# Moving one early load to another DMA queue, two 1/sqrt to ScalarE, and two pauses into a matmul fill list

## The chip, the cores and the metric

The kernel runs on one core of one Trainium2 chip. The metric is the device time of one execution in microseconds (us). Executions of one kernel differ by 1 to 2 us of 550 (549.82 to 551.59 in 20 runs of the kernel before), which is more than this change is about; so a time is given as the median of several runs and, for comparisons, as a ratio. A ratio is the mean time of one kernel's fast runs over the mean time of the other's fast runs of the same rounds on the same chip, so it is not quite the ratio of the medians quoted beside it.

Engine names in the profile: PE is TensorE (matmul), PEld its weight loads, DVE is VectorE, ACT is ScalarE, POOL is GpSimd. SPq and ACTq are the sequencers that issue DMAs on the SP and the ACT queue.

## The reference, cut to what matters

```python
xn = _layernorm(x)                      # 2048 tokens x 512
s  = attention(xn @ wq, k, v) @ wo      # 32 heads, 8 kv heads, the last 512 keys of the cache
g  = _silu(_silu(xn @ w1) @ w2)         # w1 512 x 1792, w2 1792 x 512
return x + s * g
```

## The kernel before

The tokens are worked in four blocks of 512 (four tiles of 128). At the start, block 0 is normalised and goes through the first MLP layer alone. Seven pairs of 128-wide chunks of w1 are run on tiles 0, 1 (`half` 0), then the same seven pairs on tiles 2, 3 (`half` 1):

```python
nc.sync.dma_start(x_blk[0][0:HP4, 0, :], ...)      # tile 0, half of the partitions
nc.scalar.dma_start(x_blk[0][HP4:P, 0, :], ...)    # the other half, ACT queue
# ... the same for tile 1
nc.sync.dma_start(w1_sb[0][:, :, 0 : NE // 2], ...)        # first w1 piece, 256 KB
nc.sync.dma_start(w1_sb[0][:, :, NE // 2 : NE], ...)       # second w1 piece, 256 KB
nc.scalar.dma_start(x_blk[0][:, 2:4, :], ...)              # tiles 2, 3, 256 KB, ACT queue
nc.sync.dma_start(w1_sb[0][:, :, NE:], ...)                # third w1 piece, 384 KB
nc.sync.dma_start(w1_sb[1][:, :, 0:NE], ...)               # w1's second half, 512 KB
# ... further loads, all on the SP queue
# tiles 0, 1: stats, 1/sqrt on ScalarE, center, transposes on PE
nc.scalar.activation(scratch, scratch, ACT.Tanh)   # brings the Tanh table in
stats(0, 2); stats(0, 3)
rstd_of(2, 2)                                      # 1/sqrt of tiles 2, 3 on POOL
center(0, 2); center(0, 3)
for i in range(2 * FH):
    h_pair(i, i // FH)       # 8 matmuls; then Tanh on ScalarE, multiply on VectorE
    if i == 3:               # transposes of tiles 2, 3 and their copies to xnT
        t2 = turn(2); t3 = turn(3)
        nc.scalar.copy(xnT[0][:, :, 2 * P : 3 * P], t2)
        nc.vector.tensor_copy(xnT[0][:, :, 3 * P : 4 * P], t3)
# ... queries for the first two heads are made between the last pairs
```

Then comes one long loop over 4 x 32 heads (queries, scores, exp, transposes by DMA, values). Its matmuls are interleaved with "fill" units taken from a list: the rest of the MLP while block 0 runs, the output projection later.

```python
fill = []
for b in range(NBLK):
    hs, os_ = mlp_units(b, lambda i: "f")   # first layer (4 units a chunk), second layer (14 a tile)
    fill += hs * (b > 0) + os_
def pump(n):
    for _ in range(n):
        if fill:
            fill.pop(0)(); done += 1
```

The first unit of each chunk needs one of two PSUM buffers ("f"), which comes free when VectorE has evacuated what was in it: the chunk before the last or, for the first chunks of block 1, a tile of block 0's second layer (its result is `gate`).

The softmax here doesn't subtract the row's maximum and nothing guards it: scores larger than these inputs give would overflow.

## Time and profile before

| | before |
|---|---|
| median of 20 runs | 550.57 us (549.82 to 551.59) |
| the profiled run, its span | 551.54 us, 549.3 us |
| first MLP matmul starts | 7.34 us |
| first score matmul starts (the long loop begins) | 23.09 us |
| last matmul starts | 545.24 us |

From the page of the kernel before (busy time of each engine, share of the span, instructions):

```profile
span 549.3 us, 8536 instructions
...
PE 543.1 (99%) x2676; PEld 261.7 (48%) x2676; DVE 458.5 (83%) x1258; ACT 392.3 (71%) x1125; POOL 20.7 (4%) x41
...
PE 96%; DMA 1%; DVE 1%; SPq 0%; issue 0%; ACT 0%
```

PE is the bound; the last line is the chain of work that ended last. A small change can only win where PE stands still. The waits of PE in the same trace (engine, line, what it waited for: us in all, times, longest):

```profile
PE warm_ps L635 <- DVE eps L74: 1.2, 1, 1.2
PE h_ps L683 <- DMA w_0_111<-in_B_w_dram: 1.0, 1, 1.0
PE h_ps L148 <- DVE gate_414 L190: 0.2, 1, 0.2
```

"Busy" ends of matmuls are modelled, so I measure waits from start to start: a 512-column matmul starts 0.216 us after the one before (0.108 for 256 columns), and what a start is later than that is called a *gap* below. Two stretches of the timeline of the kernel before (start, duration, engine, line, what, count, and in brackets the idle time before it with what ended it):

```profile
1.97 0.61 ACTq L617 DMA_DIRECT2D x_119<-in_A_x_dram  x1
2.25 0.59 SPq L615 DMA_DIRECT2D w_0_111<-in_B_w_dram  x1
...
3.98 0.51 SPq L619 DMA_DIRECT2D w_1_112<-in_B_w_dram  x1
...
7.31 1.28 ACT L667 ACT_TABLE_LOAD   x1
7.34 0.68 DVE L109 BATCH_NORM_STATS2 st<-x_119 128x6 f32<-128x512 bf16 x1
7.34 1.91 PE L683 MATMUL h_ps<-xnT_107,w_0_111 128*128 128x256 bf16 x16
...
8.71 1.17 ACT L691 ACTIVATE th<-h_ps 128x512 bf16<-128x512 f32 x2
9.13 0.23 POOL L114 TENSOR_SCALAR rstd<-mv 128x2 f32<-128x2 f32 x1 [7.82 <-DVE mv L110]
9.44 0.72 POOL L115 TENSOR_TENSOR rstd<-rstd,neg_half 128x2 f32<-128x2 f32 x1
...
10.23 1.49 PE L683 MATMUL h_ps<-xnT_107,w_0_111 128*128 128x256 bf16 x12 [0.98 <-DMA w_0_111<-in_B_w_dram]
...
13.61 0.42 DVE L702 COPY xnT_107<-t_ps 128x512 bf16<-128x512 bf16 x1
...
15.24 3.22 PE L683 MATMUL h_ps<-xnT_107,w_0_111 128*128 128x256 bf16 x28
...
42.53 0.38 PE L148 MATMUL h_ps<-xnT_108,w_0_111 128*128 128x512 bf16 x1
43.08 0.38 PE L148 MATMUL h_ps<-xnT_108,w_0_111 128*128 128x512 bf16 x1 [0.18 <-DVE gate_414 L190]
43.30 0.38 PE L233 MATMUL sc_ps<-kT_91,qT 128*128 128x512 bf16 x1
```

At 10.23 PE has waited for the third w1 piece (gap 1.15 us); at 11.72 for w1's second half (gap 0.17). At 43.08 the second chunk of block 1 has waited for a PSUM buffer (0.55 us since the start before it, so a gap of 0.34). One more gap, 0.18 us, is at 112.98. From 11.84 us to the last matmul no other gap is longer than 0.06 us. The matmuls of the second half (15.24) need the two copies of tiles 2, 3, which are done in time.

### The profile page before, as it was taken

The page shows a single profiled execution, that of the slowest core. Times are in us where ns is not written, and L with a number is a line of the kernel's source. Part 1 is how long each engine was busy: PE and PEld are TensorE (multiplying, and loading weights), DVE is VectorE, ACT ScalarE, POOL GpSimd, SP SyncE. Part 2 cuts the span into 40 slices and gives each one's busy share as a digit, 9 for nine tenths or more (in the row PEclk, how much of TensorE's full clock was granted, in tenths as well). Part 3 has the DMA queues.
Part 4 walks back from the last instruction along what each step waited for, and adds up shares of the span by engine and source line. Part 5 has one row for each costly group of instructions (what it writes and reads, how often), then busy time and mean ns, then how long its engine had stood idle before and what let it go on. Part 6 is the DMA issues. An engine that isn't in the chain of part 4 may idle for free.

```text
span 549.3 us, 8536 instructions
## 1 busy us (share of the span) xinstructions
PE 543.1 (99%) x2676; PEld 261.7 (48%) x2676; DVE 458.5 (83%) x1258; ACT 392.3 (71%) x1125; POOL 20.7 (4%) x41
## 2 busy tenths in 40 slices
PE   8999999999999999999999999999999999999997
PEld 5644444444444444444444444444444444444586
DVE  5878878977786688898889888988889889988897
ACT  5558757866786677777777777777788888888600
POOL 1000010000000000010001000100010000100010
PEclk9999999999999999999999999999999999999999
DMA  8969669697759799979887988797878878988931
GB/s 257 257 114 201 144 133 175 147 166 141 165 97 184 172 220 218 204 152 184 165 147 157 183 161 146 155 191 156 151 158 181 153 153 157 189 153 154 173 78 39
DMA packets 298925, 89.69 MB, mean 163 GB/s; under 512 B 282368, under 2 KB 297984, under 8 KB 298880
## 3 DMA queue, kind: packets, MB, share of 16 engines
q1 hardware_dynamic: 297136, 85.09, 79.0%
q0 software_dynamic: 1312, 3.67, 2.6%
q10 hardware_dynamic: 432, 0.39, 0.3%
q8 instruction: 21, 0.34, 0.2%
q14 instruction: 24, 0.20, 0.1%
HBM read 17.30 MB, written 2.10 MB: 35 GB/s over the span
## 4 chain that ended last, share of the span: by engine, by line
PE 96%; DMA 1%; DVE 1%; SPq 0%; issue 0%; ACT 0%
PE o_ps L275 20%; PE q_ps L211 20%; PE sc_ps L233 20%; PE s_ps L332 15%; PE oB_ps L180 8%; PE h_ps L148 7%; PE m_ps L470 4%; PE h_ps L683 2%; DMA w_0_111<-in_B_w_dram 1%; DVE gate_414 L190 0%; DVE p_all L248 0%; DVE st L109 0%; SPq L612 0%; DVE qT L223 0%; SPq L615 0%
## 5 line engine op out<-in xcount | busy, mean ns | idle before, releaser
L236 ACT ACTIVATE p_all<-sc_ps 128x512 bf16<-128x512 f32 x512 | 305.3, 597 | 104.4 <-PE sc_ps L233 100.4
L248 DVE TENSOR_SCALAR p_all<-p_all,rden 128x512 bf16<-128x512 bf16 x512 | 157.9, 351 | 9.1
L281 DVE CAST oT<-o_ps 128x512 bf16<-128x512 f32 x128 | 88.2, 689 | 35.8 <-PE o_ps L275 35.2
L236 ACT ACTIVATION_READ_ACCUMULATOR p_all<-sc_ps 128x1 f32 x512 | 100.3, 196 | 0.0
L233 PEld LDWEIGHTS <-qT 128*128 128x128 bf16 x512 | 50.1, 98 | 60.8 <-issue 0.5
L223 DVE CAST qT<-q_ps 128x512 bf16<-128x512 f32 x111 | 76.3, 687 | 3.2 <-PE q_ps L211 3.2
L332 PEld LDWEIGHTS <-oT 128*128 128x128 bf16 x384 | 37.6, 98 | 45.3
L246 DVE RECIPROCAL rden<-den 128x2 f32<-128x2 f32 x256 | 40.5, 158 | 11.2 <-ACT p_all L236 11.0
L158 ACT ACTIVATE th<-h_ps 128x512 bf16<-128x512 f32 x42 | 25.0, 595 | 4.0 <-PE h_ps L148 3.9
L332 PE MATMUL s_ps<-wo_big_2085,oT 128*128 128x512 bf16 x84 | 26.0, 379 | 0.0
L332 PE MATMUL s_ps<-wo_big_2345,oT 128*128 128x512 bf16 x84 | 26.0, 379 | 0.0
L332 PE MATMUL s_ps<-wo_big_2346,oT 128*128 128x512 bf16 x84 | 26.0, 379 | 0.0
L332 PE MATMUL s_ps<-wo_big_2084,oT 128*128 128x512 bf16 x84 | 26.0, 379 | 0.0
L233 PE MATMUL sc_ps<-kT_91,qT 128*128 128x512 bf16 x64 | 24.3, 379 | 0.0
L233 PE MATMUL sc_ps<-kT_92,qT 128*128 128x512 bf16 x64 | 24.3, 379 | 0.0
L233 PE MATMUL sc_ps<-kT_93,qT 128*128 128x512 bf16 x64 | 24.3, 379 | 0.0
L233 PE MATMUL sc_ps<-kT_94,qT 128*128 128x512 bf16 x64 | 24.3, 379 | 0.0
L233 PE MATMUL sc_ps<-kT_95,qT 128*128 128x512 bf16 x64 | 24.3, 379 | 0.0
L233 PE MATMUL sc_ps<-kT_96,qT 128*128 128x512 bf16 x64 | 24.3, 379 | 0.0
L233 PE MATMUL sc_ps<-kT_97,qT 128*128 128x512 bf16 x64 | 24.3, 379 | 0.0
L233 PE MATMUL sc_ps<-kT_98,qT 128*128 128x512 bf16 x64 | 23.9, 379 | 0.0
L349 POOL DMA_DIRECT2D out_dram<-x_e x12 | 6.6, 549 | 313.9 <-DVE rden L246 257.6
(316 smaller groups left out, 872.3 us busy)
## 6 DMA issues: line engine op xcount, KB each, us to landing
pT<-p_all SPq DMA_TRANSPOSE x128, 4.4
x_e<-in_A_x_dram POOLq DMA_DIRECT2D x12, 128.0 KB, 3.3
out_dram<-x_e POOLq DMA_DIRECT2D x12, 128.0 KB, 2.2
w_0_113<-in_B_w_dram SPq DMA_DIRECT2D x1, 896.0 KB, 10.2
w_1_114<-in_B_w_dram SPq DMA_DIRECT2D x1, 896.0 KB, 9.5
w_0_111<-in_B_w_dram SPq DMA_DIRECT2D x2, 256.0 KB, 4.2
w_1_112<-in_B_w_dram SPq DMA_DIRECT2D x1, 512.0 KB, 7.7
x_131<-in_A_x_dram SPq DMA_DIRECT2D x1, 512.0 KB, 10.6
```

What stands on the lines that cost most here:

```text
L148: nc.tensor.matmul(h_ps[:, lo : lo + n], w1_sb[f // FH][:, c, (f % FH) * P : (f % FH + 1) * P], xnT[b][:, c, lo : lo + n], start=(c == 0), ...
L158: nc.scalar.activation(th, h_ps, ACT.Tanh, scale=0.5)
L180: nc.tensor.matmul(cur["ps"], hT[b][f // 2][:, f % 2, j * P : (j + 1) * P], w2_sb[f // FH][:, f % FH, :], start=(f == 0), stop=(f == NFC - 1),
L211: nc.tensor.matmul(cur["ps"], wq_sb[h // REP][:, c, (h % REP) * DH : (h % REP + 1) * DH], xnT[b][:, c, :], start=(c == 0), stop=(c == ND - 1),
L223: nc.vector.tensor_copy(qT[s], cur["ps"])
L233: nc.tensor.matmul(sc, qT[s][:, j * P : (j + 1) * P], kT[h // REP], start=True, stop=True)
L236: nc.scalar.activation(p_all[s][:, :, j, :], sc.rearrange("p (kc q) -> p kc q", q=P), ACT.Exp, scale=INV_SQRT_DH, accum_out=den[s][:, j : ...
L246: nc.vector.reciprocal(rden, den[s][:, j0 : j1 + 1])
L248: nc.vector.tensor_scalar_mul(p_all[s][:, :, j, :], p_all[s][:, :, j, :], rden[:, j - j0 : j - j0 + 1])
L275: nc.tensor.matmul(cur["ps"], v_sb[h // REP][:, kc, :], pT[s][:, kc, :], start=(kc == 0), stop=(kc == NKC - 1))
L281: nc.vector.tensor_copy(oT[s // 2][:, s % 2, :], cur["ps"])
L332: nc.tensor.matmul(acc[j], oT[(b * HQ + h) // 2][:, h % 2, j * P : (j + 1) * P], wo_of(h), start=(h == 0), stop=(h == HQ - 1),)
```

## The change

The intent, as I read it: let the first two w1 pieces arrive undisturbed by tiles 2, 3; since those then come late, take their 1/sqrt on ScalarE, for which the Tanh table has to come in behind it (a load of 1.28 us); and fill the wait at 43 us with a score matmul.

```diff
-        nc.scalar.dma_start(x_blk[0][:, 2:4, :], x0v[:, 2:4, :])
+        nc.sync.dma_start(x_blk[0][:, 2:4, :], x0v[:, 2:4, :])
 ...
-        nc.scalar.activation(scratch, scratch, ACT.Tanh)
         stats(0, 2)
         stats(0, 3)
-        rstd_of(2, 2)
-        center(0, 2)
-        center(0, 3)
+        for j in range(2, 4):
+            rstd_first(j)
+            center(0, j)
+        nc.scalar.activation(scratch, scratch, ACT.Tanh)
 ...
-            fill += hs * (b > 0) + os_
+            if b > 0:
+                fill += hs[:ND] + [None] * 2 * (b == 1) + hs[ND:]
+            fill += os_
 ...   # pump: a None takes a turn and runs nothing
```

More of the change, by code (lines that the diff above doesn't have):

```diff
@@ L721, in pump @@
                 if fill:
-                    fill.pop(0)()
+                    u = fill.pop(0)
                     done += 1
+                    if u is not None:
+                        u()
         wo_plan = {
```

## The prediction

> **What bounds the kernel.** PE: the page gives PE 543.1 of 549.3 us (99%), the chain of waits is 96% PE, and full-width matmuls follow each other every 0.215 us. In the timeline PE loses time in four places: start-up until the first MLP matmul at 7.34 us; 1.25 us between starts at 10.23, where the waits name the third w1 piece (landed 10.18); about 0.17 us extra at 11.72 (first piece of w1's second half, landed 11.68); and 0.34 us extra at 43.08, where the second h chunk of block 1 waits for a gate on DVE that ends at 43.03. The change can win under 2 us of 550.
>
> **What the change does.**
> 1. x tiles 2, 3 (256 KB) leave the ACT queue (issued 1.97, landed 5.23) and go behind the second w1 piece on the SP queue. The first two w1 pieces (landed 6.08, 7.43) come some tenths earlier, but PE did not wait for them. The third piece and the next have the same bytes ahead of them as before. The Trainium skill ("DMA: Bandwidth & Descriptors", rules for kernel authors) says that spreading DMAs over issuing engines brings no bandwidth, since they share 16 DMA engines; the trace agrees (DMA share 1.05, 341 GB/s from 7.3 to 12.6 us). I expect 10.2 and 11.7 us again, within 0.3: the 1.25 us wait stays. x tile 1 (landed 4.28) may land 0.1 to 0.25 earlier, which lengthens that wait by as much.
> 2. Tiles 2, 3 now land at about 7.5 to 8.1 us; DVE took them up at 7.34 anyway, so their statistics start 0.2 to 0.7 later.
> 3. Two POOL operations (0.23 + 0.72 us) go; two ScalarE activations of 0.29 us come. The centred tiles are ready near 10.3 us (before: 10.94); PE transposes them only at 12.17: no gain.
> 4. The Tanh table load (1.28 us) moves from 7.31 to behind the second 1/sqrt, about 9.8 to 10.1. The first MLP Tanh moves from 8.71 to about 11.4. Four Tanh/DVE pairs at 0.6 + 0.69 us then run before the copies of the transposed tiles; the DVE copy ends near 15.1 to 15.5 (before: 14.03), and PE needs it at 15.24. Loss 0 to 0.4 us, say 0.15.
> 5. The pauses put one score matmul (0.215 us) between the first and second h chunk of block 1. The 0.34 us stall shrinks to about 0.1: gain about 0.2. The order of fills against exponentials shifts by two slots; there PSUM buffers come free 0.05 to 0.4 us before use: small stalls may come or go: +-0.2.
>
> **Sum.** -0.2 (pause) + 0.15 (late table) - 0.15 (start-up, order) = -0.2: **550.5 us, 80% range 549.6 to 551.3.** Chances: faster by over 2% 0.005, within 2% 0.99, slower by over 2% 0.005.
>
> **What the profile would show.** Step 1: PE waits for the third w1 piece until 10.0 to 10.5 and starts the next piece's weights at 11.5 to 12.0. Step 2: statistics of tile 2 start at 7.5 to 8.1, behind a DMA wait. Step 4: table load near 10, first Tanh near 11.4; a PE gap of up to 0.4 us near 15.3 blamed on an xnT copy. Step 5: PE wait at the gate near 43 us at most 0.15 us.
>
> **What would make it wrong.** If the separate ACT queue slowed the weights (the slowest DMA engine finished the third w1 piece 1.2 us after the other fifteen), the piece could come earlier and win up to 1 us. If x lands after 8.5, the Tanh chain is later still and PE stalls over 0.5 us. If the shifted order stalls every turn of block 1's h chunks, 0.5 us more is lost.

## The result, and the profile after

The full change ran in 551.08 us (median of 10 runs, 550.66 to 552.33) against 550.57 us (20 runs): ratio 1.0012, 95% interval 1.0004 to 1.0021. It is within 2%, and slightly slower: about 0.66 us (0.0012 x 550.57). From the page of the changed kernel:

```profile
span 549.5 us, 8535 instructions
...
PE 542.7 (99%) x2676; PEld 261.1 (48%) x2676; DVE 458.6 (83%) x1258; ACT 392.1 (71%) x1127; POOL 19.5 (4%) x39
...
PE 97%; DVE 1%; DMA 1%; ACT 1%; SPq 0%; issue 0%; ACTq 0%
```

The waits of PE after the change:

```profile
PE warm_ps L635 <- DVE eps L74: 1.2, 1, 1.2
PE h_ps L683 <- DMA w_0_111<-in_B_w_dram: 0.9, 1, 0.9
PE h_ps L683 <- DVE xnT_107 L702: 0.6, 1, 0.6
PE h_ps L683 <- DMA w_1_112<-in_B_w_dram: 0.2, 1, 0.2
```

The wait for the gate is no longer listed; a wait for the copy of tile 3 (L702) is new. The timeline of the changed kernel, the lines that answer to those above:

```profile
2.24 0.59 SPq L615 DMA_DIRECT2D w_0_111<-in_B_w_dram  x1
...
3.44 0.51 SPq L617 DMA_DIRECT2D x_119<-in_A_x_dram  x1
...
4.50 0.51 SPq L619 DMA_DIRECT2D w_1_112<-in_B_w_dram  x1
...
6.55 1.91 PE L683 MATMUL h_ps<-xnT_107,w_0_111 128*128 128x256 bf16 x16
8.20 0.69 DVE L109 BATCH_NORM_STATS2 st<-x_119 128x6 f32<-128x512 bf16 x1 [1.67 <-DMA x_119<-in_A_x_dram]
...
9.34 1.49 PE L683 MATMUL h_ps<-xnT_107,w_0_111 128*128 128x256 bf16 x12 [0.88 <-DMA w_0_111<-in_B_w_dram]
...
9.94 0.30 ACT L118 ACTIVATE rstd<-mv,eps 128x1 f32<-128x1 f32 x1 [0.50 <-DVE mv L110]
10.26 1.28 ACT L672 ACT_TABLE_LOAD   x1
...
11.66 1.07 ACT L691 ACTIVATE th<-h_ps 128x512 bf16<-128x512 f32 x2
...
14.89 0.42 DVE L702 COPY xnT_107<-t_ps 128x512 bf16<-128x512 bf16 x1
...
15.36 3.23 PE L683 MATMUL h_ps<-xnT_107,w_0_111 128*128 128x256 bf16 x28 [0.62 <-DVE xnT_107 L702]
...
42.67 0.38 PE L148 MATMUL h_ps<-xnT_108,w_0_111 128*128 128x512 bf16 x1
42.88 0.38 PE L233 MATMUL sc_ps<-kT_91,qT 128*128 128x512 bf16 x1
43.22 0.38 PE L148 MATMUL h_ps<-xnT_108,w_0_111 128*128 128x512 bf16 x1
...
91.78 0.38 PE L233 MATMUL sc_ps<-kT_94,qT 128*128 128x512 bf16 x1
92.14 0.38 PE L148 MATMUL h_ps<-xnT_109,w_0_111 128*128 128x512 bf16 x1
```

At 42.88 the score matmul stands in the old hole, and the next chunk starts 0.34 us later: the gap has shrunk from 0.34 to 0.13 us. At 92.14 a new gap of 0.14 us has opened (0.36 after the start before it): the chunk waits for a PSUM buffer whose evacuation ends at 92.08. It comes back as 0.18 us at 97.50 and at 102.86.

PE's gaps of the two traces, worked out from the starts of all matmuls, account for the difference in span (+0.24 us):

| where | before | after | difference |
|---|---|---|---|
| start-up to the first MLP matmul | 3.14 | 2.34 | -0.80 |
| third w1 piece | 1.15 | 1.05 | -0.10 |
| w1's second half | 0.17 | 0.40 | +0.23 |
| copies of tiles 2, 3 | 0 | 0.79 | +0.79 |
| gate near 43 us | 0.34 | 0.13 | -0.21 |
| new waits, 92 to 103 us | 0 | 0.50 | +0.50 |
| wait near 113 us | 0.18 | 0 | -0.18 |
| sum of these | | | +0.23 |

Part of the start-up row is PE's clock. The first ten warm-up matmuls start 0.43 us apart in both traces (1.18 to 5.00 us). The transposes behind them still start 0.107 us apart in the trace of before, and 0.056 in the other. The Trainium skill ("TensorE: Matmul & The Clock Gate", Part 1) says that the array runs at half rate until about 3.4 us of activity release it, by a window that runs freely, so that the moment varies from run to run. The traces agree that the moment varies, though the slow pace lasts longer here: it ends by 5.33 us in the changed kernel's trace and not before 6.78 in the other, 4.1 and 5.6 us after the first warm-up matmul. In the fourteen traces the first MLP matmul starts anywhere from 6.54 to 7.34 us, and neither front is always the earlier. (The clock is not all of it: in e4_scalar the transposes are fast but start late, and in e14_full_w1act the matmul waits for the first w1 piece.)

The table reads as "the front gained 0.9 and gave 1.0 back". But +0.24 us in one pair of traces is not the 0.66 us of the runs, and the profiled run of before took 551.54 us, the slow end of what its 20 runs took. A single trace is one draw of a scattered quantity. So each experiment below was timed in five rounds, and its trace served as a further sample.

Four quantities from the trace make the samples comparable. The *loop* is the time from the start of the first score matmul to that of the last matmul. The *first score* is the start of the long loop. The span is the sum of the two and 4.02 us, within 0.01, in every trace. The *landing* is the last of the 16 completions of the load of w1's second half, and *KB by 8 us* what the packets of the SP and ACT queues that were finished by then had moved (1 KB is 1024 bytes). Two windows show the loop (stretch, its length, then busy time of each engine): first of the kernel before,

```profile
23.09:545.24 522.15, 521.95 (x2529) 247.28 (x2528) 441.53 (x1221) 380.12 (x1104) 19.00 (x32) 1.00 0.82 160
```

then of the changed kernel:

```profile
23.23:545.48 522.25, 522.21 (x2529) 247.25 (x2528) 441.93 (x1221) 379.60 (x1104) 18.82 (x32) 1.00 0.82 160
```

### The profile page after: what moved, and what is told of

The parts are those of the page before. It is cut to its first block, busy times and chain, and to the rows that moved or that the text cites. A ratio compares the mean times of both kernels' runs of the same rounds, so it can differ in the third digit from the quotient of the medians.

```text
span 549.5 us, 8535 instructions
## 1 busy us (share of the span) xinstructions
PE 542.7 (99%) x2676; PEld 261.1 (48%) x2676; DVE 458.6 (83%) x1258; ACT 392.1 (71%) x1127; POOL 19.5 (4%) x39
## 3 DMA queue, kind: packets, MB, share of 16 engines
q0 software_dynamic: 1312, 3.67, 2.5%
## 4 chain that ended last, share of the span: by engine, by line
PE 97%; DVE 1%; DMA 1%; ACT 1%; SPq 0%; issue 0%; ACTq 0%
PE sc_ps L233 20%; PE q_ps L211 20%; PE o_ps L275 20%; PE s_ps L332 15%; PE oB_ps L180 9%; PE h_ps L148 7%; PE m_ps L470 4%; PE h_ps L683 1%; DMA x_119<-in_A_x_dram 1%; DVE st L109 0%; ACT L672 0%; ACT th L691 0%; SPq L612 0%; DVE hT_0_194 L692 0%; DVE hT_2_196 L692 0%
## 5 line engine op out<-in xcount | busy, mean ns | idle before, releaser
L275 PE MATMUL o_ps<-pT,v_105 128*128 128x512 bf16 x64 | 18.4, 379 | 0.0
```

The lines of the kernel that those rows point to most:

```text
L275: nc.tensor.matmul(cur["ps"], v_sb[h // REP][:, kc, :], pT[s][:, kc, :], start=(kc == 0), stop=(kc == NKC - 1))
```

## The experiments

All outputs are right. The traces of these runs lack 48 of the 2676 matmul records, each of which leaves a hole of exactly one matmul; such holes are not counted as gaps. The first four ran on one chip together, the next four on the same chip later, the last four on another. Times are medians of five runs, against nine of the kernel before in the same rounds.

| run | tiles 2, 3 | 1/sqrt, table | pauses | time, before | ratio (95%) | landing | KB by 8 us | first score | loop |
|---|---|---|---|---|---|---|---|---|---|
| before, first trace | ACT | POOL, early | no | | | 11.68 | 1465 | 23.09 | 522.15 |
| after, first trace | SP | ScalarE, late | yes | 551.08, 550.57 | 1.0012 (1.0004 to 1.0021) | 11.01 | 1459 | 23.23 | 522.25 |
| e1_front | SP | ScalarE, late | no | 551.12, 550.21 | 1.0011 (0.9998 to 1.0023) | 10.88 | 1412 | 22.70 | 522.15 |
| e2_pause | ACT | POOL, early | yes | 550.91, 550.21 | 1.0008 (0.9995 to 1.0021) | 10.72 | 1518 | 22.14 | 522.25 |
| e3_queue | SP | POOL, early | no | 551.17, 550.21 | 1.0014 (1.0000 to 1.0027) | 11.36 | 1364 | 22.78 | 522.15 |
| e7_copies | SP | ScalarE, late | yes | 552.20, 550.21 | 1.0030 (1.0017 to 1.0042) | 11.39 | 1335 | 23.96 | 522.26 |
| e4_scalar | ACT | ScalarE, late | no | 550.46, 550.44 | 0.9999 (0.9985 to 1.0013) | 10.79 | 1478 | 22.24 | 522.15 |
| e11_w1act | SP, w1 on ACT | POOL, early | no | 550.30, 550.44 | 1.0002 (0.9989 to 1.0014) | 10.39 | 1497 | 21.81 | 522.15 |
| e8_before | ACT | POOL, early | no | 550.35, 550.44 | 0.9999 (0.9986 to 1.0011) | 10.27 | 1517 | 21.68 | 522.15 |
| e9_after | SP | ScalarE, late | yes | 551.41, 550.44 | 1.0016 (1.0003 to 1.0028) | 11.92 | 1410 | 23.34 | 522.25 |
| e10_comp | ACT | POOL, early | made good | 549.94, 550.57 | 0.9990 (0.9976 to 1.0003) | 10.37 | 1538 | 21.78 | 521.93 |
| e12_w1act_comp | SP, w1 on ACT | POOL, early | made good | 550.53, 550.57 | 1.0002 (0.9989 to 1.0014) | 10.81 | 1491 | 22.23 | 521.93 |
| e13_xfirst | SP, ahead of w1 | POOL, early | no | 550.58, 550.57 | 1.0005 (0.9992 to 1.0018) | 11.20 | 1321 | 22.61 | 522.15 |
| e14_full_w1act | SP, w1 on ACT | ScalarE, late | yes | 550.60, 550.57 | 1.0005 (0.9993 to 1.0018) | 9.99 | 1577 | 22.32 | 522.25 |

### The halves apart

The front half alone (the edit is the first two hunks of the change):

> Only the front half of the change: tiles 2, 3 on the SP queue behind the second w1 piece, 1/sqrt on ScalarE, Tanh table behind it; no pauses. Theory A (sum of PE gaps of the two traces): the weights land 0.7 us earlier, the wait for the xnT copy gives back 0.8 us, so 0 +-0.3 us against before, with a PE gap of 0.7 to 0.9 us near 15.4, the old 0.34 gap near 43 and the old single 0.18 gap near 113 us. Rival B (the earlier weights are an accident of one profile, since one straggling DMA engine set both landings): 0.5 to 0.8 us slower than before, with the third w1 piece landing again near 10.2. Rival C (the shifted fill order alone is the loss): at least 0.3 us faster than the full change.

Measured: ratio 1.0011, so theory A's 0 within 0.3 us is missed in the mean. The gap before the second half was 0.40 us at 14.83, smaller than expected. The third w1 piece landed at 9.05, earlier than in before's first trace, so rival B's 10.2 is not seen; its time, 0.6 us (0.0011 x 550), is. Rival C falls in the mean: the front alone is no faster than before. (The interval, 0.9998 to 1.0023, is -0.1 to +1.3 us, so the time alone settles little.)

The pauses alone (the last hunk of the change):

> Only the two pauses. Theory A: gap near 43 us falls from 0.34 to about 0.13 (-0.2 us), three new gaps of 0.14 to 0.18 us between 90 and 105 (+0.5), the gap near 113 goes (-0.18): +0.1 us, so a ratio of 1.0002. Rival C: the pauses are the whole loss, +0.5 us or more. If the new gaps near 92, 97 and 103 are not here, they came from the front half instead.

Measured: every gap as theory A has it: 0.12 us at 42.13, then 0.14, 0.18 and 0.18 at 91, 96 and 102, none near 112. The loop is 522.25 us, 0.10 us longer than in every trace without pauses. So the new waits come from the pauses, and the pauses cost 0.10 us net. The timed ratio, 1.0008, is unclear and adds nothing. More telling is its front, which is that of the kernel before: the first score came at 22.14 instead of 23.09. The early part of the same code scatters by a microsecond; the "gain" of 0.9 us in the table of gaps was a slow draw of before.

### The parts of the front

The queue move alone:

```diff
-        nc.scalar.dma_start(x_blk[0][:, 2:4, :], x0v[:, 2:4, :])
+        nc.sync.dma_start(x_blk[0][:, 2:4, :], x0v[:, 2:4, :])
```

> Only the move of tiles 2, 3 to the SP queue; 1/sqrt stays on POOL and the Tanh table loads early as before. Theory A: weights as early as in the full change (third piece near 9.3, next near 11.0); tiles 2, 3 are centred only near 11.9, so PE waits about 0.4 us before their transposes, but the Tanh chain starts near 8 us and the gap near 15.4 is at most 0.2 us: 0.1 to 0.4 us faster than before. Rival B: weights near 10.2 and 11.7 and no gain.

Measured: ratio 1.0014, five runs between 551.09 and 551.31. This is a miss of theory A, which had it faster than before. The third piece landed at 9.89, the second half at 11.36, nearer to rival B than to theory A, and the only gaps before the loop were the two DMA waits. PE did not wait for the transposes, because the weights were later than tiles 2, 3. The queue move alone is as slow as the whole front. The first line of its waits of PE:

```profile
PE h_ps L683 <- DMA w<-in_B_w_dram: 1.3, 1, 1.3
```

The ScalarE part alone (the second hunk of the change, tiles 2, 3 still on the ACT queue):

> Only the ScalarE part: 1/sqrt of tiles 2, 3 on ScalarE and the Tanh table behind it; tiles 2, 3 stay on the ACT queue, no pauses. Theory D1 (the late Tanh table costs time by itself, since VectorE's multiply chain behind it is 0.7 us a pair against 0.87 us of matmuls and can't catch up before the copies of tiles 2, 3): weights as in the kernel before, first Tanh near 10.8 to 11.0 instead of 8.7, a PE gap of 0 to 0.4 us before the second half's matmuls: 0 to 0.4 us slower than before. Theory D2 (the loss is the queue move alone): no gap and no difference.

Measured: ratio 0.9999, with a gap of 0.02 us before the second half. With tiles 2, 3 early, the late table costs next to nothing.

The queue move with the first w1 piece in its old place on the ACT queue:

```diff
-        nc.sync.dma_start(w1_sb[0][:, :, 0 : NE // 2], w1v[:, :, 0 : NE // 2])
+        nc.scalar.dma_start(w1_sb[0][:, :, 0 : NE // 2], w1v[:, :, 0 : NE // 2])
```

> The queue move alone as in the earlier run of it (1/sqrt on POOL, early table), but the first w1 piece is issued from the ACT queue in the place that tiles 2, 3 had left. Theory Q (the move costs because one queue starts transfers too slowly: 420 to 460 KB had moved by 4.5 us with tiles 2, 3 on SP, 490 to 520 KB with them on ACT): bytes by 4.5 us back at 480 KB or more, w1's second half lands 0.2 to 0.5 us earlier than in the move alone (11.36 there), time 0.3 to 0.6 us below it, so within 0.3 us of before. Rival (the weights wait behind the bytes of tiles 2, 3 themselves, whichever queue starts): no gain against the move alone.

Measured: ratio 1.0002, landing 10.39 instead of 11.36: in the mean the loss of the move is gone, as theory Q says. (The two runs are of different rounds and their intervals, 1.0000 to 1.0027 and 0.9989 to 1.0014, overlap; the landing says it more clearly than the time.) In PE's timeline the first 32 matmuls, those on the third piece and the first on w1's second half among them, follow each other without a break:

```profile
7.33 3.71 PE L683 MATMUL h_ps<-xnT,w 128*128 128x256 bf16 x32
```

Theory Q's stated mechanism does not hold: only 411 KB had moved by 4.5 us. By 8 us it had 1497 KB against 1364 for the move alone. So putting a load back on the ACT queue matters, but not through more bytes in the first 4.5 us.

Tiles 2, 3 on the SP queue, but ahead of the first w1 piece:

```diff
+        nc.sync.dma_start(x_blk[0][:, 2:4, :], x0v[:, 2:4, :])
         nc.sync.dma_start(w1_sb[0][:, :, 0 : NE // 2], ...)
         nc.sync.dma_start(w1_sb[0][:, :, NE // 2 : NE], ...)
-        nc.scalar.dma_start(x_blk[0][:, 2:4, :], x0v[:, 2:4, :])
```

> The kernel before, only that tiles 2, 3 are issued on the SP queue ahead of the first w1 piece instead of on the ACT queue beside it. Theory Q (one queue for all early loads moves fewer bytes, in whatever order): fewer than 1,460 KB by 8 us (before: 1,465 to 1,518; moved behind the second piece: 1,335 to 1,459), w1's second half near 11.3, ratio 1.0007 to 1.0015. Rival order theory (the place behind the second w1 piece is what costs): as before, 1.000.

Measured: 1321 KB by 8 us and a landing at 11.20: by the trace it belongs with the move, whatever the order. The timed ratio, 1.0005, reaches from no loss to the full loss and does not decide it.

### Why the late table sometimes costs

The full change, with the first four Tanh and multiply pairs held behind the copies of tiles 2, 3:

```diff
         for i in range(2 * FH):
-            h_pair(i, i // FH)
+            held.append(h_pair(i, i // FH))   # matmuls only; returns the Tanh and multiply
             if i == 3:
                 ...                           # transposes and copies of tiles 2, 3
+            if i >= 3:
+                for e in held: e()
+                held = []
```

> The full change, but the first four Tanh and multiply pairs stand behind the two copies of the transposed tiles 2, 3 in the order of ScalarE and DVE (same instructions, same arithmetic). Theory A (the late Tanh chain holds the copies back): the 0.79 us gap near 15.4 vanishes and nothing else moves: 0.6 to 0.8 us faster than the full change, 0 to 0.4 us faster than before. Rival (PE waits there for something else than the queue order, such as the arrival of x): the gap stays above 0.4 us.

Measured: the gap before the second half went from 0.79 to 0.10 us, yet this is the slowest kernel of all, 1.0030. Its waits of PE (here and below without the wait ahead of the first warm-up matmul, 1.2 us in every trace):

```profile
PE sc_ps L233 <- DVE qT L223: 0.9, 1, 0.9
PE h_ps L683 <- DMA w<-in_B_w_dram: 0.9, 1, 0.9
```

The wait moved to the first score, whose query is cast by VectorE behind the whole chain (gap 1.07 us at 23.96). Holding the pairs made the chain start at 12.79 instead of 11.66, and its eleven multiplies from 13.42 on took 7.70 us, 0.70 us each, against 0.87 us of matmuls per pair: VectorE regains 0.17 us a pair and had not caught up after fourteen. "Nothing else moves" was wrong: with the copies put first PE lost as much at the end of the chain, because the chain then began later still. That it is the late start alone is argued from this one trace, not tested.

The full change with the first w1 piece on the ACT queue (the one-line edit shown above, on top of the change):

> The full change with the first w1 piece on the ACT queue. If the queue were the only loss, the ratio falls to 1.0002 (the 0.1 us of the pauses stays). If the late Tanh chain is a second limit hidden behind the late weights, the weights' second half lands near 10.4, but PE then waits 0.3 to 0.6 us for the copies of tiles 2, 3 near 14.3: first score 22.1 to 22.4, ratio 1.0007 or so.

Measured: the weights landed at 9.99, the earliest of all, and PE waited for the copy instead, as the second alternative has it:

```profile
PE h_ps L683 <- DMA w<-in_B_w_dram: 0.4, 1, 0.4
PE h_ps L683 <- DVE xnT L702: 0.4, 1, 0.4
```

The gap at the copy is 0.58 us. (The DMA wait listed is that of the first MLP matmul, at 7.30, for the first w1 piece, which landed only at 7.26 in this trace.) So there are two limits, late weights and a late Tanh chain, and PE pays for the later one only. The repeat of the full change shows the other case:

> The full change once more: ratio to before 1.001 to 1.0015. Its trace: w1's second half lands at 10.9 to 11.4, a PE gap of 0.4 to 0.8 us before the matmuls of the second half of tokens, and 522.25 us from the first score to the last matmul (0.10 more than without pauses).

Measured: ratio 1.0016. Here the weights landed at 11.92, later than expected, and PE waited for them alone:

```profile
PE h_ps L683 <- DMA w<-in_B_w_dram: 1.7, 1, 1.7
```

No wait for the copy is left, though the table load came at 9.90, about as late as in the first trace of the change (10.26). The expected gap of 0.4 to 0.8 us was absorbed.

### Noise

> The kernel before once more, as a control of noise: ratio 1.000 within 0.001. Its trace is a third sample of the front part: first score matmul between 22.0 and 23.1 us, 11.42 us behind the landing of w1's second half, and from there to the last matmul 522.15 us as in both earlier traces of this order.

Measured: ratio 0.9999 (0.9986 to 1.0011) for the same kernel against itself. Its first score came at 21.68, below the range that I had expected, with no DMA wait of PE listed:

```profile
PE h_ps L148 <- DVE gate L190: 0.2, 1, 0.2
```

So the 1.15 us wait of before's first trace, on which the prediction dwelt, is not in every execution.

### Pauses without their side effect

The pauses, with two later slots holding two units each, so that all fill units behind them keep their old places and the list its old length (`pump` as in the change):

```diff
-            fill += hs * (b > 0) + os_
+            if b > 0:
+                if b == 1:
+                    two = [lambda u=u, w=w: (u(), w()) for u, w in zip(os_[2:6:2], os_[3:6:2])]
+                    hs, os_ = hs[:ND] + [None] * 2 + hs[ND:], os_[:2] + two + os_[6:]
+                fill += hs
+            fill += os_
```

> The kernel before with the two pauses, but two later slots of block 1's second layer hold two units each, so that every later fill unit stands where it stood before. Theory P (the pauses take 0.22 us off the wait near 43 us; the three later waits of 0.14 to 0.18 us come from the shift of the order by two slots): gap near 43 us about 0.12, no gaps near 92, 97 and 103, the old one near 112 us still there; 521.93 us from the first score to the last matmul against 522.15 in the kernel before and 522.25 with plain pauses. Rival (the gaps near 92 to 103 come from the pause's place, not the later shift): they stay, 522.25. In time at most 0.2 us faster, inside the noise.

Measured: gaps of 0.12 us at 41.77 and 0.18 at 111.45, none between; the loop is 521.93 us, as expected to the last digit. The waits near 92 to 103 us are therefore the price of the later shift, not of the pause. The lines of this kernel's timeline that answer to those at 91.78 and 92.14 of the change have the usual spacing:

```profile
90.55 0.38 PE L233 MATMUL sc_ps<-kT,qT 128*128 128x512 bf16 x1
90.76 0.38 PE L148 MATMUL h_ps<-xnT,w 128*128 128x512 bf16 x1
```

The timed ratio is 0.9990 with an interval that holds 1: faster by 0.22 us in the loop by the trace, not shown by the clock.

Both edits together, the first w1 piece on ACT with the queue move, and the made-good pauses (1/sqrt on POOL):

> A candidate to beat both: tiles 2, 3 on SP behind the second w1 piece, the first w1 piece on the ACT queue, 1/sqrt on POOL, early table, and the compensated pauses. Sum of the single results: front as with the first w1 piece on ACT (ratio 1.000 within 0.0013 there), 0.2 us less in the loop: ratio 0.9990 to 1.0005; first score to last matmul 521.93.

Measured: loop 521.93 again, ratio 1.0002: not a version that beats before. Of all kernels run, the one with made-good pauses and the old front is the only one with a mean below before by more than 0.01%, and no kernel beats it beyond doubt.

## Why the prediction was right or wrong

The range (549.6 to 551.3) holds the measured 551.08 us, and "within 2%" was right. The sign was not: 0.2 us faster was predicted, about 0.66 us slower measured. That the range holds says little for the steps: it is 1.7 us wide, more than the whole effect.

- **PE bound, under 2 us to win:** held; the loop of 522 us differed by 0.10 us and the rest happened in the first 24 us.
- **Step 1, the queue move: the step that failed.** I argued that the third piece and the next have the same bytes ahead of them and so land as before, within 0.3 us. Over the eight traces with an early load of weights or of tiles 2, 3 on the ACT queue, w1's second half lands at 10.63 us in the mean (9.99 to 11.68); over the six with all of these on SP, at 11.29 (10.88 to 11.92). That is 0.66 us later, though the ranges overlap. KB by 8 us do not overlap: 1465 to 1577 against 1321 to 1459, means of 1510 and 1384. In the ten traces in which the Tanh chain held PE by no more than 0.02 us the first score follows the landing by the same 11.41 to 11.45 us of work, so there the delay is paid in full. Timed: the move alone 1.0014, the move with a w1 piece put on ACT 1.0002, with intervals that overlap. *Why* the weights land later is open: my first idea, a slower start, failed on its own number (411 KB by 4.5 us). The move lets the ACT queue run dry at 3.1 to 3.3 us, against 4.6 to 6.8 in the other eight traces. It also makes SP issue one load more, at about 0.5 us each, ahead of w1's second half, which is so issued at 4.48 to 4.50 us in the six traces and at 3.67 to 3.98 in the eight. No run separates the two. What speaks against the issue time alone is that these loads had all been issued by about 5.0 us, while the KB moved still overlap at 5.5 us (719 to 757 against 700 to 812) and part only by 7.0 us (1052 to 1170 against 1182 to 1248). What happens inside the queues is not shown.
- **The targets themselves** (10.2 and 11.7 us) were read from one trace. The same code gave landings of the second half from 10.27 to 11.68 in four traces of the unchanged front, so a claim of 0.3 us could not have been tested on one pair. That pair even pointed the wrong way, 0.67 us earlier. Much of the scatter is one late completion: the load counts as landed with the last of its 16, which came 0.5 to 2.2 us behind their median (2.07 in before's first trace: 11.68 against 9.61). The medians differ less and scatter less: 9.42 to 9.67 in the eight traces, 9.68 to 10.21 in the six, 0.36 us later in the mean; so about half of the 0.66 us is in all completions and the rest in the last one.
- **Steps 2 and 3:** tiles 2, 3 were taken up at 8.20 behind a DMA wait (7.5 to 8.1 predicted) and centred at 10.69 (10.3); no gain from it, as said.
- **Step 4, the late table:** the mechanism was right: table load at 10.26, first Tanh at 11.66, copy done at 15.31, a gap blamed on that copy. The size was off: 0.79 us in the first trace, 0.40 in the front alone, 0 in the repeat, where 0.15 (at most 0.4) was predicted. I held the copy against 15.24, PE's time in the trace of before; where the weights come earlier, PE needs it at 14.57 (15.36 less the gap). It is not a cost to add but the larger of two limits, and the mean loss of the whole front is about that of the queue move alone (1.0011 and 1.0014).
- **Step 5, the pauses:** the wait shrank from 0.34 to 0.13 us as predicted (0.34 to 0.1). The order shift, put at 0 within 0.2 us, cost 0.32 us (three waits of 0.50 in all against 0.18 that went). Net +0.10 us instead of -0.2.
- **The sum:** about +0.6 us for the front by the timed runs and +0.10 for the pauses by the traces agree with the measured +0.66 (the front's interval alone is -0.1 to +1.3 us). The predicted -0.2 lacked the landing and had the order shift at zero.

## What to carry to other kernels

Weights "with the same bytes ahead" of them can still land later when another load is moved to their queue: here by 0.66 us in the mean, whether through the emptied second queue or the later issue. Test such a move against several traces, since the first 20 us of one kernel scattered by more than the whole effect. Where two late things meet at one consumer, cost the later of the two, and read its need from the new schedule, not from the old one. A pause that fixes one wait shifts everything behind it: put the slots back after the hole, and check that the later starts are where they were.

## What the Trainium skill lacked or had wrong

- "DMA: Bandwidth & Descriptors", Rules for kernel authors: it says of spreading DMAs over the issuing engines that it doesn't help bandwidth and only saves sequencer issue time. Here the loads of the first microseconds moved 1465 to 1577 KB by 8 us on two queues and 1321 to 1459 on one, and w1's second half landed 0.66 us later in the mean on one. This does not show the page wrong: the issue of that load also moved by 0.5 us or more (4.48 to 4.50 us against 3.67 to 3.98), and no run tells the two apart. What the page lacks is a case of a short burst that starts from idle, in which the place of a load among the issuing engines is worth that much.
- "ScalarE: Activation LUTs", What ACT_TABLE_LOAD costs: the load took 1.28 us here, as the page has it. Of the further drain of about 1.38 us that it adds to each switch nothing is to be seen: the load at 10.26 starts behind an activation that ends at 10.24, and the next activation starts 0.01 us after the load ends (11.54, 11.55).
- No page that I used tells how far one kernel's early DMA landings scatter between executions: 10.27 to 11.68 us for one load in four traces of the same front.
